# A recurrent attention with a gated feed-forward: checks of the decay weights in halves with buffers of their own, and a new table of the issue order

## The chip, the core and the metric

The kernel runs on one core of one Trainium2 chip. The core has five engines that run side by side, each through a queue of its own in order: TensorE (PE; its weight loads are listed as PEld), VectorE (DVE), ScalarE (ACT), GpSimd (POOL) and SyncE (SP), which here issues all transfers. The metric is the device time of one execution, in microseconds. Three runs of the kernel before gave 365.49 (median), 364.83 and 368.83.

## The reference

B = 4, H = 8 heads, S = 768 steps, D = 48 channels; then a feed-forward of width 1024.

```python
for t in range(S):                      # per batch and head, state is D x D
    kt, vt, rt, wt = k[:, :, t], v[:, :, t], r[:, :, t], w[:, :, t]
    cur = einsum('bhd,bhe->bhde', u * kt, vt)
    y[:, :, t] = einsum('bhd,bhde->bhe', rt, state + cur)
    state = wt[..., None] * state + einsum('bhd,bhe->bhde', kt, vt)
x = y as (B, S, H * D)
h = relu(x @ w_in); u, v = halves of h
v_n = (v - mean(v)) / sqrt(var(v) + 1e-6)
v_s = w_spatial @ v_n + b_spatial       # over the 768 steps
out = (u * v_s) @ w_out
```

## The kernel before

The 768 steps of a batch are cut into 6 chunks of 128; the 4 x 6 chunks are the slots 0 to 23. A slot turns its decays W into cumulative products with two scans on VectorE (F backwards at line 434, E forwards at line 440, which is written into a PSUM tile pa), scales k with F and r with E (lines 448 and 450), forms the 128x128 scores of all heads on TensorE (pa, line 493), copies them under a mask into As, whose diagonal holds the bonus term (line 498; the diagonal is made by line 474 on GpSimd or 479 on ScalarE), and sums its output y in PSUM (pyw, line 533): first from As and v, then from the state Sd of the slots before. The state goes on over a transposed k (pt, line 513), a product pd (line 571), two sums S0 and S1 (lines 579 and 583) and copies Sd (line 587). y is split into a high and a low part xT for the feed-forward, whose products are all made of three matmuls of such parts (`mm3`, lines 613 to 615): ph is the half v of h, pu the half u, pv the product with w_spatial, po the output. Between them lie the normalization (hv, line 680, on VectorE or ScalarE), splits into vh and vl (lines 683 and 685), and t, gh and gl (lines 719 to 724).

The weights come as raw 64-bit numbers. `split64` takes them apart: a multiplication, a shift (`low`; on VectorE line 335), a `join` (line 339) and a `sign` (line 343) on VectorE, a cast and a difference (line 351). w_spatial is split as well (lines 301 and 303).

From slot 6 on the diagonal comes from a tile N, which holds r and k of a chunk in natural order: N*N and N*u are products of lines 456 and 458, dg a sum of line 459. In slots 0 to 5 it comes from a product rk (line 414, in the same buffer N) and a small matmul pg (line 421).

The fast form is valid while no decay is over 1 and no cumulative product too small. `check_w` reads each of the 16 groups of decays once more and lets ScalarE sum what lies over 1 into a column of `over`; `range_check` at the end folds `over` and the products `prod` into one number `bad`, which decides whether a slow general form runs afterwards. With these inputs it doesn't run.

The order is no scheduler's. `Program.op` collects about 1800 operations with the engines each may run on and what it reads and writes. `plan` then takes them from a table of words PLAN: a letter for the engine (T, V, A, G, S) and the operation's number in base 36, or F and a count of filling matmuls (`warm`, line 818). The numbers beside the letters at each `op` call (0.45 for a load, say) are costs for whoever makes such a table; `plan` uses only that the letter is among them. Buffers are taken where an operation is issued; a tile whose buffer is still in use waits for its last reader. Tag N has one buffer, W, kr and v two each.

Of the kernel before, what the change touches and what calls it, by code (L numbers as in the profile page):

```python
# [19 lines left out]
G = H // 2  # L20
# [14 lines left out]
A73 S7s V6x V6y G6z G7a T7d V70 G74 S1i T3x S8u A5y T5z V7w A7e V1z A1u G28 S33 V7c T75 S7t A60 V76 V20 G1v T8b
S29 V8c A72 T61 A51 T62 V7x A52 A3y G7u V77 A7b T63 A3z G81 T7f A40 V7y A1j G82 T7g T7h A64 A65 V7z V80 V83 A7i
T7v S8v T8g V84 G8d A8e T7j V8z G86 T88 G87 A7k V1k V1l S30 S8w A8h A85 T7l Sep A53 T7m V89 A66 V1m A94 T7n A21
V90 V8a T9e G8x T8i T8j A1n A7o S3a V8f T8y V1o V97 T8k Sad G95 A7p A7q A8l V9f G9a V91 A67 A31 Seq V69 Tbd G68
V92 G6a A2a G99 V22 V93 Ses S3 A3b A35 Tal V96 G9g A9i V6b G6c Taz T8m A8n Aae G6d Tbe Vet Veu Saf Tam Tan G32
T9b S2f G6e V6f G98 Tb0 Tb1 A6g Tbr V6i Sfn Tbs V6l Aey A6j Gez V9d V9c Tbt Ab2 G6h A6m Gf4 Abu Tbf V9h G6k Aao  # L40
S3o Tfa A34 Vfb S3h T9j Aag T9k Sah T9l V36 Tg8 V37 V3c A9m V6n Vg9 A2g Sfo T8o Abg Vew T9n T8p A24 V3d G25 A9o
A38 Vev Vex T8q A8r T9p G2b S4 V3e Vfr V39 Td1 A8s T9q T9r A2m A8t S2u Vf0 G2n Aai Tcn V3j V3i A9s Tco A9t Tcp
Tdt Saj V3k Gfx S2c A9u Tf7 G9w Tdu V2h S2i V3l A3f A9v V9x A3q V3p Vfs Tdf V9y V9z Tdv Tdg A2v G3g Sgs Acq Va0
Va1 Va2 Va9 Va3 Aak G2w Ser Td2 Aaa Td3 Aa4 Tdh V3r Tb3 V3s Gab Adw Va5 Adi A2d Sgr S2x Tac Tb4 Vfu A3m V2e A3t
Ad4 Tb5 G3u Tbh Tgd V3n Tbi S2o Aa6 A2j Age Tbj Vf1 Tb6 Tbk Aa7 Tbv S2r Vf2 Vf3 Tap Taq Sfp Tbw Va8 V2k A2p Gf5
Vf8 Tbl Tar Gf6 Vft Sib A2s Vfv G2t G2q Tas Vfy A2y Sfq Gfz Gg0 Vf9 Tbx Tby Tb7 Tb8 Tbz G2z Tc0 Vb9 Tbm Vba Tat
Vc1 Tcr Vg1 Sgt Vbn Gc2 Ag3 Tau Abb Vav Tfc Vbo Abp Gfw Vgv Gga Tfd Gg4 Thc Vbq Tg5 Afe Agc Ac3 Gaw Sgu Agb Tcs
Vhd Tct Gh1 Tcu Aax Tff Vg7 Afg Vay Vbc Tcv Gc4 Tcw Tfh Gg2 Vgw Vcx Tfi Vg6 Vgx Tfj Afk Gh3 Gh4 Tch Vh5 Tci Tcj
Tck Sid Vgy Vh2 Ah7 Tgf Gh8 Vh0 Sje Tgg Tgh Sie Vcl Th9 Agz Vif Agi Vig Sic Vhe Tgj Gin Afl Afm Vhb Gio Aiq Gcy
# [137 lines left out]
def dve(n):  # L187
    return 0.157 + n / 960
# [755 lines left out]
```

## Time and profile before

| | |
|---|---|
| median of three runs | 365.49 us |
| the profiled execution | 369.64 us |
| its span, first to last instruction | 367.9 us |
| TensorE busy | 353.3 us, 3978 matmuls |
| VectorE busy | 255.7 us |
| ScalarE busy | 184.1 us |
| GpSimd busy | 165.3 us |
| DMA traffic | 47.66 MB, 130 GB/s mean |

The profile is of one execution. Matmuls are pipelined and the ends of single ones are modelled, so the distance from start to start tells more than a duration. A wait is put down to what ended last before it.

### The profile page before, as it was taken

Reading aid. Unit: us, or ns where it says so; the run is one execution under the profiler, and the core shown is the slowest. Engines: PE = TensorE matmul, PEld = TensorE weight load, DVE = VectorE, ACT = ScalarE, POOL = GpSimd, SP = SyncE. Lnnn points to the kernel's source line nnn. Section 1 sums busy time; section 2 is a strip of 40 time slices with the busy share of each in tenths; the row PEclk is TensorE's granted clock in tenths of the full one; section 3 lists DMA queues with packets and bytes.
Section 4 is the critical chain, followed back from the end, with each engine's and each line's share of the span. In section 5 each row is a group of like instructions: output and inputs, shape, how many; then the busy total and the mean of one; then the engine's idle time right before and its main releaser. Section 6 shows DMA issues by size and latency. Waiting matters only on the chain.

```text
span 367.9 us, 9774 instructions
## 1 busy us (share of the span) xinstructions
PE 353.3 (96%) x3978; PEld 324.5 (88%) x3978; DVE 255.7 (69%) x465; ACT 184.1 (50%) x482; POOL 165.3 (45%) x211
## 2 busy tenths in 40 slices
PE   7889897999999999999999999999999999999995
PEld 7766686999898988998799989999889899999994
DVE  5989998999977873788967498667696424424041
ACT  3588775874445557403465646622544564713121
POOL 5769582769557251716634164412334104114110
PEclk9999998999999999999999999999999999999998
DMA  7877767653265553352554545253404232000101
GB/s 210 249 240 201 210 203 239 205 172 116 73 201 161 154 161 131 103 151 59 142 173 122 160 142 166 69 172 87 130 2 138 66 94 79 21 23 0 62 26 70
DMA packets 30065, 47.66 MB, mean 130 GB/s; under 512 B 2896, under 2 KB 21456, under 8 KB 30016
## 3 DMA queue, kind: packets, MB, share of 16 engines
q1 hardware_dynamic: 30016, 47.00, 42.4%
q8 instruction: 32, 0.52, 0.6%
q14 instruction: 17, 0.14, 0.1%
HBM read 42.27 MB, written 4.72 MB: 128 GB/s over the span
## 4 chain that ended last, share of the span: by engine, by line
PE 75%; DVE 10%; issue 3%; DMA 1%; POOL 0%; ACT 0%; DVEq 0%; POOLq 0%; SPq 0%
PE pv L613 9%; PE pv L615 9%; PE pv L614 9%; PE pyw L533 8%; PE pa L493 5%; PE po L613 5%; PE po L615 5%; PE po L614 5%; PE pu L613 3%; PE pu L615 3%; PE pu L614 3%; PE ph L613 3%; PE ph L615 3%; PE ph L614 3%; DVE Sd L587 2%
## 5 line engine op out<-in xcount | busy, mean ns | idle before, releaser
L613 PE MATMUL pv<-ws,vh 128*128 128x384 f32 x192 | 65.0, 338 | 0.0
L615 PE MATMUL pv<-ws,vl 128*128 128x384 f32 x192 | 64.3, 335 | 0.0
L614 PE MATMUL pv<-ws,vh 128*128 128x384 f32 x192 | 64.2, 335 | 0.0
L498 DVE COPY_PREDICATED As<-mask,pa 128x512 f32<-128x512 int32 x48 | 34.6, 733 | 10.6 <-PE pa L493 8.3
L719 DVE TENSOR_TENSOR t<-pv,b_sb 128x384 f32<-128x384 f32 x32 | 17.6, 549 | 32.3 <-PE pv L615 19.9
L721 POOL TENSOR_TENSOR t<-t,us 128x384 f32<-128x384 f32 x19 | 21.1, 1113 | 37.2 <-DVE t L719 31.9
L474 POOL TENSOR_SCALAR_AFFINE_SELECT As<-dg 128x512 f32<-128x512 f32 x33 | 25.7, 785 | 26.1 <-PE pyw L533 12.7
L613 PEld LDWEIGHTS pv<-ws,vh 128*128 128x128 f32 x192 | 36.1, 188 | 0.8 <-issue 0.2
L614 PEld LDWEIGHTS pv<-ws,vh 128*128 128x128 f32 x192 | 36.1, 188 | 0.4
L615 PEld LDWEIGHTS pv<-ws,vl 128*128 128x128 f32 x192 | 36.0, 188 | 0.0
L613 PE MATMUL pu<-xT,wi 128*128 128x384 f32 x96 | 33.5, 348 | 0.0
L613 PE MATMUL po<-wo,gh 128*128 128x384 f32 x96 | 33.0, 344 | 0.0
L615 PE MATMUL pu<-xT,wi 128*128 128x384 f32 x96 | 32.4, 338 | 0.0
L615 PE MATMUL po<-wo,gl 128*128 128x384 f32 x96 | 32.3, 337 | 0.0
L614 PE MATMUL po<-wo,gh 128*128 128x384 f32 x96 | 32.3, 336 | 0.0
L614 PE MATMUL pu<-xT,wi 128*128 128x384 f32 x96 | 32.2, 336 | 0.0
L434 DVE TENSOR_TENSOR_SCAN F<-zz,W 112x512 f32<-112x512 f32 x24 | 29.1, 1215 | 3.5 <-DMA W<-in_tr_dram 1.9
L723 ACT CAST gh<-t 128x384 fp32r<-128x384 f32 x32 | 16.2, 510 | 30.1 <-POOL t L721 19.7
L440 DVE TENSOR_TENSOR_SCAN pa<-zz,W 112x512 f32<-112x512 f32 x24 | 29.4, 1223 | 0.3
L613 PE MATMUL ph<-wi,xT 128*128 128x512 f32 x72 | 29.4, 408 | 0.0
L615 PE MATMUL ph<-wi,xT 128*128 128x512 f32 x72 | 28.5, 395 | 0.7 <-DVE xT L608 0.7
L614 PE MATMUL ph<-wi,xT 128*128 128x512 f32 x72 | 28.3, 393 | 0.0
(185 smaller groups left out, 845.6 us busy)
## 6 DMA issues: line engine op xcount, KB each, us to landing
kr<-in_tr_dram SPq DMA_DIRECT2D x23, 448.0 KB, 4.3
N<-in_nat_dram SPq DMA_DIRECT2D x18, 384.0 KB, 3.3
Nw<-in_gt_dram SPq DMA_DIRECT2D x16, 384.0 KB, 3.1
W<-in_tr_dram SPq DMA_DIRECT2D x24, 224.0 KB, 3.6
v<-in_nat_dram SPq DMA_DIRECT2D x24, 192.0 KB, 3.6
out_dram<-ot SPq DMA_DIRECT2D x24, 192.0 KB, 2.0
wst<-in_w_spT_dram SPq DMA_DIRECT2D x12, 192.0 KB, 4.4
d_('wv', 0)_157<-in_w_in_dram SPq DMA_DIRECT2D x1, 512.0 KB, 7.2
```

The lines of the kernel that those rows point to most:

```text
L434: op({"V": 1.24}, lambda: nc.vector.tensor_tensor_scan(flat(F()[:R])[:, ::-1], flat(zz[:R])[:, ::-1], flat(W())[:, ::-1], 0.0, ALU.max, AL ...
L440: op({"V": 1.24}, lambda: nc.vector.tensor_tensor_scan(flat(E()[:R]), flat(zz[:R]), flat(W()), 0.0, ALU.max, ALU.mult), r=[(W, 0), ("zz", ...
L474: e.affine_select(out=As(), in_=dg()[:, j::2].unsqueeze(2).broadcast_to([P, G, C]), pattern=[[0, G], [1, C]], compare_op=ALU.is_equal, fil ...
L493: nc.tensor.matmul(pa[j]()[:, g, :], kk()[rs, g, :], rr()[rs, g, :], start=True, stop=True)
L498: op({"V": 0.725}, lambda j=j, As=As: nc.vector.copy_predicated(As(), mask.unsqueeze(1).broadcast_to([P, G, C]), pa[j]()), r=[(pa[j], 0)], ...
L533: nc.tensor.matmul(py()[Q * n:Q * (n + 1), k_, :], a, b, start=n not in started, stop=not left[0], skip_group_check=True)
L613: nc.tensor.matmul(ps, ah, bh, start=first, stop=False)
L614: nc.tensor.matmul(ps, ah, bl, start=False, stop=False)
L615: nc.tensor.matmul(ps, al, bh, start=False, stop=last)
L719: op({"V": dve(HT)}, lambda: nc.vector.tensor_tensor(t1(), pv()[:, :HT], b_sb[:, tsl], ALU.add), r=[(pv, 0), ("b", 0)], w=[(t1, 0)])
L721: op({"V": dve(HT), "G": pool(HT)}, lambda e: e.tensor_tensor(t1(), t1(), us(), ALU.mult), r=[(us, 0)], w=[(t1, 0)], port=True)
L723: op({"A": act(HT)}, lambda: nc.scalar.copy(gh(), t1()), r=[(t1, 0)], w=[(gh, 0)])
```

## The change

Three things. First, `check_w` loads each group as two halves of 128 x 384 in place of one of 128 x 768, into a tag of its own, Nw, with two buffers in another pool, and checks each half by itself; `over` has 32 columns for it. In the program's list a group's check now follows one of the slots 7 to 22, one group to a slot, and no longer comes in fours behind the last slot of a batch; the table places the halves where it likes. Second, some costs beside operations have other values. Third, the table is new from its first word to its last, with other engines for some operations.

```diff
-    over = cp.tile([P, B * G], F32, name="over")
+    over = cp.tile([P, 2 * B * G], F32, name="over")
...
     def check_w(n):
-        w = buf(p2, [P, 2, DM], "N", f"Nw{n}", 1)
-        def flat():
-            return w().rearrange("p a d -> p (a d)")
-        load(w, [0], lambda: nc.sync.dma_start(flat(), gt[n, :, 0, :]), P * S * 4)
-        op({"A": 1.03}, lambda: nc.scalar.activation(flat(), flat(), AF.Relu, bias=neg, accum_out=over[:, n:n + 1]),
-           r=[(w, 0)], w=[(w, 0), ("over", n)])
+        for h in range(2):
+            w, m = buf(pm, [P, HT], "Nw", f"Nw{n}_{h}", 2), 2 * n + h
+            load(w, [0], lambda w=w, h=h: nc.sync.dma_start(w(), gt[n, :, 0, h * HT:(h + 1) * HT]), P * HT * 4)
+            op({"A": 0.7}, lambda w=w, m=m: nc.scalar.activation(
+                w(), w(), AF.Relu, bias=neg, accum_out=over[:, m:m + 1]), r=[(w, 0)], w=[(w, 0), ("over", m)])
...
-        op({"T": 0.89}, mm, r=[(kr, 0), (kr, 1)], w=[(pa[0], 0), (pa[1], 0)], mode="rows")
+        op({"T": 0.98}, mm, r=[(kr, 0), (kr, 1)], w=[(pa[0], 0), (pa[1], 0)], mode="rows")
...
+        if 0 < i - B_PE <= B * G:
+            check_w(i - B_PE - 1)
         if c == NC_ - 1:
-            for g in range(G):
-                check_w(b * G + g)
...
-T0 Sq Vw Vx Vy A11 Sr Ss S2 St S1 S41 S42 S5 A15 Gu S43 G12 Fd Tv A14 S54 Vz V13 F3 T18 A10 V46 A16 G17 V19 T1b
+Sq Sr Ss S1 T0 Vw Gu A11 S2 S41 Vx Vy G12 Fb Tv St S5 Vz S42 S43 A14 S54 V13 G16 G17 A10 G15 V46 F3 T18 V19 T1b
```

Three places of the order. In the names the first number of As, kr, pa, F, W and dg is the slot; hv and vl carry batch and chunk. In the changed file, lines behind `check_w` have numbers smaller by 3, lines between the table and `check_w` larger by 1.

VectorE, from the E scan of slot 5 to the masked copies of slot 5, before:

```order
L440 SCALAR_TENSOR_TENSOR pa5_0_885<-zz_80,W5_612 112x512
...
L450 TENSOR_TENSOR kr5_744<-kr5_744,pa5_0_885 112x4x127
L667 TENSOR_TENSOR st0_0_667<-st0_0_667 128x3
L434 SCALAR_TENSOR_TENSOR F6_934<-zz_80,W6_786 112x512
L438 RECIPROCAL zz_80<-F6_934 112x4
L680 TENSOR_SCALAR hv0_0_674<-hv0_0_674,st0_0_667 128x512
L680 TENSOR_SCALAR hv0_1_666<-hv0_1_666,st0_0_667 128x512
L680 TENSOR_SCALAR hv0_2_719<-hv0_2_719,st0_0_667 128x512
L498 COPY_PREDICATED As5_1_883<-mask_103,pa5_1_947 128x512
L498 COPY_PREDICATED As5_0_901<-mask_103,pa5_0_885 128x512
L587 COPY Sd_113<-S1_112 48x4x48
```

and now:

```order
L437 SCALAR_TENSOR_TENSOR pa5_0_945<-zz_80,W5_644 112x512
L677 TENSOR_SCALAR hv0_0_590<-hv0_0_590,st0_0_591 128x512
L447 TENSOR_TENSOR kr5_701<-kr5_701,pa5_0_945 112x4x127
L677 TENSOR_SCALAR hv0_1_606<-hv0_1_606,st0_0_591 128x512
L584 COPY Sd_113<-S1_112 48x4x48
L453 TENSOR_TENSOR N6_885<-N6_885 128x384
L495 COPY_PREDICATED As5_0_950<-mask_103,pa5_0_945 128x512
L336 TENSOR_SCALAR d_('wo', 1)_834<-d_('wo', 1)_834 128x384
L495 COPY_PREDICATED As5_1_926<-mask_103,pa5_1_965 128x512
L336 TENSOR_SCALAR d_('wo', 2)_904<-d_('wo', 2)_904 128x384
L456 TENSOR_REDUCE dg6_1019<-N6_885 128x8
L431 SCALAR_TENSOR_TENSOR F6_1023<-zz_80,W6_775 112x512
```

The F scan of slot 6 has moved behind the copies of slot 5; two hv stand apart in place of three together; Sd, N*N of slot 6 and a shift have come in front of the last copy.

GpSimd at the same place, before:

```order
L303 TENSOR_TENSOR ws1_122<-wst5_1_775,ws0_121 128x384
L670 TENSOR_TENSOR st0_0_667<-st0_0_667 128x3
L466 COPY vp1_116<-v5_777 128x4x2x16
L448 TENSOR_TENSOR kr6_889<-kr6_889,F6_934 112x4x127
L685 TENSOR_TENSOR vl0_0_990<-hv0_0_674,vh0_0_966 128x512
L466 COPY vp0_115<-v6_905 128x4x2x16
L685 TENSOR_TENSOR vl0_1_1000<-hv0_1_666,vh0_1_981 128x512
```

and now:

```order
L667 TENSOR_TENSOR st0_0_591<-st0_0_591 128x3
L471 AFFINE_SELECT As5_0_950<-dg5_868 128x512
L304 TENSOR_TENSOR ws1_122<-wst2_1_758,ws0_121 128x384
L682 TENSOR_TENSOR vl0_0_977<-hv0_0_590,vh0_0_952 128x512
L455 TENSOR_TENSOR N6_885<-N6_885,u_sb_107 128x384
L682 TENSOR_TENSOR vl0_1_1008<-hv0_1_606,vh0_1_974 128x512
L471 AFFINE_SELECT As6_1_1041<-dg6_1019 128x512
L445 TENSOR_TENSOR kr6_937<-kr6_937,F6_1023 112x4x127
```

The product on kr6 has moved from the front of both vl to behind them, and N6 comes between the vl.

SyncE's queue, where the first checks are loaded, before:

```order
L375 DMA W6_786<-in_tr_dram 112x4x128
L310 DMA d_('wo', 1)_841<-in_w_out_dram 128x768
L392 DMA Nw0_876<-in_gt_dram 128x768
L378 DMA kr6_889<-in_tr_dram 112x1024
L383 DMA v6_905<-in_nat_dram 128x384
L846 DMA u_sb_107<-in_u_rep_dram 128x384
L392 DMA Nw1_937<-in_gt_dram 128x768
```

and now:

```order
L376 DMA W5_644<-in_tr_dram 112x4x128
L389 DMA Nw6_0_648<-in_gt_dram 128x384
L384 DMA v4_657<-in_nat_dram 128x384
L379 DMA kr5_701<-in_tr_dram 112x1024
L843 DMA u_sb_107<-in_u_rep_dram 128x384
L384 DMA v5_753<-in_nat_dram 128x384
...
L376 DMA W6_775<-in_tr_dram 112x4x128
...
L383 DMA N6_885<-in_nat_dram 128x768
```

A half of group 6 is loaded first, a slot earlier than a check was before, and N6 is loaded before any other check stands in the queue.

## Rows read from the trace of the kernel before

**Rows 1.** Busy time by windows: window, then PE, PEld, DVE, ACT, POOL, clock, DMA

```profile
30.00:40.00 10.00, 8.12 (x131) 5.91 (x127) 9.94 (x13) 6.76 (x21) 7.86 (x9) 1.00 0.70 205
100.00:150.00 50.00, 50.00 (x592) 45.36 (x589) 34.55 (x69) 28.98 (x78) 22.84 (x34) 1.00 0.53 157
```

**Rows 2.** TensorE's waits: engine, line, releaser; total us, times, longest

```profile
PE pyw L533 <- DVE As L498: 4.6, 3, 2.7
...
PE pyw L818 <- ACT xT L606: 0.6, 1, 0.6
```

**Rows 3.** Timeline, VectorE, then TensorE: start, us, engine, line, operation [idle before]

```profile
51.99 5.33 DVE L680 TENSOR_SCALAR hv<-hv,st 128x512 f32<-128x512 f32 x3
57.25 1.32 DVE L498 COPY_PREDICATED As<-mask,pa 128x512 f32<-128x512 int32 x2
...
58.62 0.66 PE L533 MATMUL pyw<-As,v 128*32 128x128 f32 x8 [2.69 <-DVE As L498]
```

**Rows 4.** Timeline of GpSimd meanwhile, first and last of the four

```profile
53.08 1.27 POOL L448 TENSOR_TENSOR kr<-kr,F 112x508 f32<-112x508 f32 x1
...
55.78 1.26 POOL L685 TENSOR_TENSOR vl<-hv,vh 128x512 fp32r<-128x512 f32 x1
```

**Rows 5.** Granted clock in tenths, forty slices; two pieces of the chain (start, us)

```profile
PEclk9999998999999999999999999999999999999998
...
58.62 3.21 PE pyw L533 x56
...
97.73 1.67 PE pyw L533 x56
```

**Rows 6.** Timeline of TensorE around a change of matmul form; a transposition in the chain

```profile
50.60 0.33 PE L614 MATMUL pu<-xT,wi 128*128 128x384 f32 x1
50.78 0.34 PE L615 MATMUL pu<-xT,wi 128*128 128x384 f32 x1
51.05 1.16 PE L493 MATMUL pa<-kr 48*128 48x128 f32 x16
...
76.77 0.39 PE pt L513 x4
```

**Rows 7.** VectorE by groups (count, busy us, mean ns, idle before); two rows of its timeline

```profile
L434 DVE TENSOR_TENSOR_SCAN F<-zz,W 112x512 f32<-112x512 f32 x24 | 29.1, 1215 | 3.5 <-DMA W<-in_tr_dram 1.9 <-POOL kr L448 0.7 <-issue 0.6
L587 DVE COPY Sd<-S 48x192 f32<-48x192 f32 x18 | 12.4, 691 | 0.8 <-POOL S L583 0.5
L680 DVE TENSOR_SCALAR hv<-hv,st 128x512 f32<-128x512 f32 x13 | 11.7, 922 | 0.0
L438 DVE RECIPROCAL zz<-F 112x4 f32<-112x4 f32 x24 | 4.3, 178 | 0.2
L456 DVE TENSOR_TENSOR N<-N 128x384 f32<-128x384 f32 x6 | 3.9, 651 | 3.2 <-DMA N<-in_nat_dram 3.2
L583 DVE TENSOR_TENSOR S<-S,prod 112x192 f32<-112x192 f32 x6 | 2.6, 438 | 0.0
...
42.08 0.40 DVE L335 TENSOR_SCALAR d_('wu', 0)_607<-d_('wu', 0)_607 128x512 int32<-128x512 int32 x1
59.23 0.56 DVE L339 SCALAR_TENSOR_TENSOR e_('wo', 0)_910<-e_('wo', 0)_910,d_('wo', 0)_623 128x384 int32<-128x384 int32 x1
```

**Rows 8.** The check on ScalarE (ns least, median, most); SyncE's waits for its buffer

```profile
L393 ACT ACTIVATE Nw<-Nw,neg x16: 923/936/944, 52.0 to 333.2; 128x768 f32<-128x768 f32 x16
L393 ACT ACTIVATION_READ_ACCUMULATOR Nw<-Nw,neg x16: 182/186/209, 52.9 to 334.0; 128x1 f32 x16
...
SPq L392 <- ACT Nw L393: 28.8, 10, 3.9
```

**Rows 9.** Timeline of VectorE: first, longest and last of ten lengthened instructions

```profile
13.91 0.97 DVE L339 SCALAR_TENSOR_TENSOR e_('wv', 0)_267<-e_('wv', 0)_267,d_('wv', 0)_157 128x512 int32<-128x512 int32 x1
...
32.88 2.28 DVE L339 SCALAR_TENSOR_TENSOR e_('wu', 2)_537<-e_('wu', 2)_537,d_('wu', 2)_445 128x512 int32<-128x512 int32 x1
...
46.27 1.57 DVE L351 TENSOR_TENSOR wi<-e_('wu', 0)_696,wi 128x512 fp32r<-128x512 f32 x1
```

More of the change, by code (lines that the diff above doesn't have):

```diff
@@ L35 @@
[L35 to L49, printed above, removed]
@@ new lines @@
+Sy7 Vl9 Tnh Vqj Tja Gqv Al4 Tni Tmb Tmc Ajb Ale Vke Tnj Vqk Tmd Ank Vl8 Gqp Vql Tkf Ay8 Ame Vqm Vqo Vqq Tkg Tkh
+Vrs Vld Gdy Vqn Vrt Vru Tlf Gqu Vrk Gqw Tlg Srj Aki Grv Vrl Ssn Tlh Ali Akj Grw Tqx Tr0 Vr1 Vlj Vqz Srh Tdz Te0
+Ssp Te1 Grq Grp Vqy Vrm Avh Ajc Te2 Tlk Ajd Tll Tlm Sub Su7 Tr2 Aln Vrn Vrr Grx Tr3 Ts1 Vs2 Try Alo Gs3 Vs0 Ar4
+Akk Tor Tos Vr5 Gsz Vrz Alp Alq Vlr Gt0 Tot Tr6 Vls Aou As5 Glt Teb Sso Vlu Tr7 Glv Glw Vlx Vt1 Tec Aly Vm4 Ted
+Gt3 Am5 Te5 Sud Am1 Ve3 Te6 Se4 Te7 Tr8 Am2 Vm3 Alz Vm6 Gm0 Gun Tee Swn Te8 Aef Ar9 Vs4 Tmf Ara Au8 Tmg Tmh Tmi
@@ new lines @@
+T197 T10a T101 V10b A18d Ssl V19b V18e T17a A194 A195 T102 T103 T104 T11n T11o T11p T11q T11r T11s T119 V105
+G19c T11a V198 S106 A19e A19d G15u G15v T10v Asm V11t V15w V15x V15y A164 T10w T10x T10y G196 V199 Sm7 A161 A162
+A17b A17c A17d T10z T110 V163 A15z G160 T11b T11c T11d T11e V111 T19f T19g T19h G11u A19i T10r V10q V19j T10s
+T10t A11v A10u V11f T1al T19k G11w A165 T19l T19m T18f T18g A19n G11g T18h T129 A11h V11i A19o A19p G112 T1am
+T1a7 A113 A18i T1an V114 T12a A18j A18k S10c T1a8 T1a9 A1aa T11x T12b A19q T1d1 A1ao T1d2 T1d3 A1d4 V19s G19t
@@ new lines @@
+G19r G19u V19v T123 G19w V19x A1a1 A1a4 A1a5 V166 G1a6 A19y T11y T11z T120 T124 A1a2 A121 T125 V1a3 T12c A19z
+G1a0 A17h S14j T126 V127 T1ab T1b3 A12d T1b4 T1b5 S122 S128 A14k S12e T1bh Sm9 T1az T1ac T1ad T1ae T1af T1b0
+T1b1 T1b6 T1ag A1b2 T1ap T1aq T1ar T1bi T1bj T1bk V1ah T1bl T1b7 T1bm T1b8 T1cn T1as T1co G1ai V1b9 V1bn T1at
+V1bo A1bp V1bq A1aj T1cp T1df G1ak T1au V1av A1cq T1c9 Ama T1ca V1aw A1ax V1ay T1c3 T1cd T1ce T1dg V1ba A1bb
+T1cf T1cg V1bc T1dh A1di T1c4 T1cb T1br T1c5 A1cc T1c6 T1bs T1bx T1bt T1bu Am8 V1ec A1c7 T1by S1c8 T1ch T1ci
@@ L99 @@
+V1cj T1bz T1c0 T1dj T1dk V1ck T1dl A1cl T1dm T1cr G1cm T1cs A1bv S1bw T1dn T1do V1dp T1d5 G1dq T1ct T1cu T1cv
+A1dr T1cw V1cx V1cy V1ds T1d6 A1cz V1d0 T1d7 T1d8 T1d9 A1c1 S1c2 T1da T1e5 T1e6 T1dz T1e0 V1db V1dc A1dd V1de
+T1dt T1du T1dv T1dw T1e1 V1dx T1e2 S1dy T1e7 T1e8 A1e3 S1e4 V1e9 A1ea T1ed S1eb V1ee
 """
@@ L343, in sign @@
             V.scalar_tensor_tensor(m, dh, -2**31, m, ALU.bitwise_and, ALU.bitwise_or)
-        op({"A": act(n), "V": one}, rebias, r=[(d, 0)], w=[(em, 0)], port=True)
-        op({"A": act(n), "V": one}, low, w=[(d, 1)], port=True)
+        op({"A": act(n) + 0.06, "V": one}, rebias, r=[(d, 0)], w=[(em, 0)], port=True)
+        op({"A": 0.2 + n * 0.00114, "V": one}, low, w=[(d, 1)], port=True)
         op({"V": two}, join, r=[(d, 1)], w=[(em, 0)], port=True)
@@ L465, in slot_prep @@
         vp = q["vp"] = vps[i % 2]
-        op({"A": 0.3, "G": 0.68}, lambda e: (e.copy if e is nc.scalar else e.tensor_copy)(
+        op({"A": 0.3, "G": 0.3}, lambda e: (e.copy if e is nc.scalar else e.tensor_copy)(
             vp.rearrange("p g (a b) -> p g a b", b=T)[:, :, 0::3],
@@ L831, in low @@
             nc.vector.tensor_tensor(okr[:, 0:1], okr[:, 0:1], okr[:, 1:2], ALU.min)
-        op({"V": 0.9}, low, r=[("over", i) for i in range(B * G)] + [("Wc", i) for i in range(NS)] + [("S1",)],
+        op({"V": 0.9}, low, r=[("over", i) for i in range(2 * B * G)] + [("Wc", i) for i in range(NS)] + [("S1",)],
            w=[("okr",)] + [("Wc", i) for i in range(NS)])
```

122 lines of the change are left out of this document (60 added, 62 removed).

## The prediction

> **What bounds the kernel now.** I read the table by windows first. From 100 to 150 us TensorE is busy for 50.00 of 50 us while VectorE has 34.55; from 30 to 40 us it is VectorE that is full, 9.94 of 10 [rows 1]. So the kernel has two parts. In the first sixty microseconds the weights are still being split, and the decay scans, the masked copies and the splitting share VectorE; TensorE gets its inputs as fast as VectorE makes them. After that TensorE runs without pause to the end, so whatever the first part loses is lost for good, and whatever it gains is kept.
>
> Then the waits of TensorE, and the largest says it directly: 4.6 us in 3 waits for the masked copies As of line 498, the longest 2.7 [rows 2]. The timeline shows that one: TensorE stands still for 2.69 us and begins again at 58.62, when the two copies As of slot 5 are done. VectorE is not idle meanwhile. Its three normalizations hv of line 680 take 5.33 us together, and As follows only at 57.25 [rows 3]. An undisturbed one is far shorter: the group has 13 with 11.7 us busy [rows 7], and the ten others make (11.7 - 5.33)/10 = 0.64 us. What holds them is beside it on GpSimd: from 53.08 to 57.04 it goes through four operations without a pause, from 1.27 us on kr to a vl of 1.26 us, and VectorE gets on only behind the last [rows 4]. I call this a hold: a VectorE instruction whose operands are ready stands while GpSimd works.
>
> The stall costs twice. The page's row of granted clock, forty slices of 9.2 us, has an 8 in the seventh, which holds the stretch behind the stall, and again at the very end; all others are nines [rows 5]. In the chain the 56 small matmuls behind the stall take 3.21 us, and the same 56 take 1.67 us at 97.73 [rows 5]: TensorE worked at 1.2 GHz there and not at 2.4. The two other waits for As, 1.9 us together, did not do that. So this episode cost 2.69 + (3.21 - 1.67) = 4.2 us.
>
> The profiled execution took 369.64 us, 367.9 in its span and 1.74 around it; the median of the three runs is 365.49. Without the episode the profiled one would be at 365.4. I take it that the median runs lack it, or have it small, and that one of the three (368.83) had one.
>
> **The change part by part.** *The check loads.* Sixteen checks of 768 columns become thirty-two of 384. One now takes 0.94 us on ScalarE and 0.19 us for reading its accumulator [rows 8], 18 us in all. A half has at least half the first and the whole second, 0.66, and at most what it has now; 32 of them are 21 to 36 us. ScalarE is busy for half the span, and TensorE's longest wait for it is 0.6 us [rows 2], so I count nothing; without that cover it would be 3 us at the lower end. The buffers: SyncE waited 28.8 us in 10 waits until a check had freed the common N buffer [rows 8], and the loads of W, kr and v stood behind it in the one queue. The halves wait for each other only. A gain needs TensorE to wait for such a load, and its waits show none, so nothing again. Sixteen more issues fall to SyncE, which computes nothing.
>
> *The costs written beside the operations* are read by no one when the order comes from the table: nothing.
>
> *The table, VectorE up to the As copies of slot 5.* This is where TensorE's longest stall ended, so I count what VectorE has to do until then in either order. New in front of them: three shifts of line 335, one join and one sign of the 384-wide weights, one product N*N, one state product S. Gone: the scan F of slot 6, one copy Sd, one of the three hv and three short ones. By rows [rows 7]: 3 x 0.40 + 2 x 0.56 + 0.65 + 0.44 = 3.4 us come, and 1.21 + 0.69 + 0.64 + three of at most 0.18 = 3.0 go. These means hold average holds already. VectorE has +0.4 us more.
>
> *The table, TensorE up to the same place.* In front of As5 it has done one transposition and one third of a projection (three matmuls) less. The transposition is 0.39 us; matmuls start 0.17 us apart, so the third is 0.52 [rows 6]. These 0.9 us are still to do when it is let go: +0.9.
>
> *Changes between full matmuls and the small tiled ones.* The last full matmul before the small ones at 51.05 takes 0.27 us from start to start, others 0.17 [rows 6]: 0.1 us per change. The orders have 91 and 88 changes: -0.3.
>
> *Filling matmuls.* 31 in place of 28, all in the first 25 us, where TensorE is ahead of VectorE. I count nothing; with no cover, three of two passes of a tenth of a microsecond would be 0.6.
>
> *The long hold.* Before, three hv stand together, and behind them on GpSimd the product on kr6, a vl, a copy and the other vl are all ready. Now two hv remain there, with the product on kr5 between them; the kr6 product has moved behind As5, and GpSimd has one mask diagonal, one difference ws and one vl, after which its next product needs N6 from VectorE. So it must pause. The price lies between 0 (as long a hold) and -4.2 (gone). I take it as gone: the queue that filled those four microseconds isn't there any more.
>
> *Other holds.* From 13.9 to 46.3 us ten instructions of VectorE that read and write SBUF are longer than the shortest of their kind, from the join of 0.97 at 13.91 over one of 2.28 at 32.88 to a difference of 1.57 at 46.27, by 6.3 us in all [rows 9]. Which operation meets which is decided by tenths of a microsecond, and the new order deals all of them anew. I take the same sum; between none (-6.3) and double (+6.3) nothing is excluded.
>
> *The end.* Both orders close with the same steps: last output group, two half copies, store, check matmul. Nothing.
>
> Sum: 369.64 - 4.2 + 0.4 + 0.9 - 0.3 = 366.4 us, 0.3% over the median shown.
>
> **Rivals.** *The long hold comes back (slower).* Behind hv, Sd and N*N in the new order GpSimd can have a diagonal, ws and vl ready in a row, about 0.6 + 1.0 + 1.3 = 2.9 us, and the As copies of slot 5 stand behind all of them. For it: four instructions that can be held stand there in front of As5, where there were three. Against it: vl needs hv and a ScalarE cast first. It decides once TensorE stands as long as it did before 58.62, near 2.7 us; then the clock falls as well and the whole episode is back: 366.4 + 4.2 = 370.6 us. Slower also if the scan of slot 6, now behind As5, comes late: I count 6.0 us of VectorE work up to the next score matmul against 6.6 of TensorE work, so only 0.6 us of cover.
>
> *More instructions, more holds (slower).* The new order has five more long VectorE instructions with SBUF on both sides in front of As5 (three shifts, join, sign, N*N and S come, one Sd and one hv go). If each finds GpSimd in the middle of an operation like the 1.26 us vl [rows 4], with its busy share of 0.79 [rows 1], it loses 0.63 x 0.79 = 0.5 us, together 2.5: 368.9 us. For it: the ten holds are of that size. Against it: the shift at 42.08 took 0.40 us and the join at 59.23 0.56, no more than other undisturbed ones [rows 7]. The Trainium skill, SBUF — State Buffer, section "SBUF: two separate sides", states the rule behind this rival: VectorE and GpSimd take one pair of ports in turn as an exclusive lock, whoever starts first for its whole instruction, and the other one blocks. The trace agrees that VectorE stands while GpSimd works, and differs in the length: the long hold lasted over four instructions of GpSimd, not over one.
>
> *The holds shrink (faster).* If the new interleaving halves the 6.3 us, TensorE is let go 3.1 us earlier: 363.3. For it: more operations on ScalarE (copies Sd, the first check) keep out of the quarrel. Against it: GpSimd's work in front of As5 is the same within half a microsecond. To be faster by 1% three quarters of the holds have to go.
>
> *The check's buffers do what they are for.* If the loads behind SyncE's waits were what VectorE's waits for N and kr hang on, these vanish: 3.2 us for N in six products [rows 7]. TensorE waited for none of it, so at most the last microsecond could be won: 365.4.
>
> **How the numbers follow.** Forecast 366.4 with a chance of 0.44; the long hold returns 0.18 (370.6); more holds 0.13 (368.9); the holds shrink 0.2 (363.3); the check's buffers pay 0.05 (365.4). One per cent, about what a measurement of this kernel can tell from no change, is 361.8 to 369.1. Slower by more: the first rival and a good third of the second, 0.23. Faster by more: somewhat over half of the shrinking holds, 0.12. Between: 0.65. The range goes from 362.3, where two thirds of the holds are gone, to 370.8, the returned episode; some 0.1 are left out on each side. The likeliest case's own range is 364.5 to 368.5.
>
> **What would show it.** Right: As5 done on VectorE between 54 and 57 us; TensorE's waits for As in the first sixty microseconds under 3 us in total; granted clock at full level from the first ten microseconds to the end; behind that TensorE without pauses as before; no ScalarE or SyncE wait of TensorE through a check. The step on hv is wrong if any hv or Sd takes over 2 us before As5; the step on work is wrong if TensorE waits for the scores of slot 6 or 7; the step on the checks is wrong if TensorE waits for a load. The prediction falls if the stretch behind 60 us, and not the one before it, differs by more than 1 us between the two kernels.

## The result

The changed kernel takes 371.3 us in the median of 20 runs (370.07 to 373.95), the kernel before 368.06 in the median of its 20 runs (364.56 to 370.61): a ratio of 1.0121 with a 95% interval of 1.0096 to 1.0146, slower by 1.2% (by the two medians alone 0.9%). I had said 366.4, with a range up to 370.8 and 0.23 for slower by more than 1%. The runs of before lie six microseconds apart, some near 365 and most between 367 and 370; those of the changed kernel lie closer together.

### The profile page after: what moved, and what is told of

It reads as the page before. It is cut to its first block, busy times and chain, and to the rows that moved or that the text cites. A ratio compares the mean times of both kernels' runs of the same rounds, so it can differ in the third digit from the quotient of the medians.

```text
span 371.8 us, 9821 instructions
## 1 busy us (share of the span) xinstructions
PE 355.9 (96%) x3984; PEld 327.8 (88%) x3984; DVE 251.2 (68%) x461; ACT 186.9 (50%) x504; POOL 165.7 (45%) x216
## 4 chain that ended last, share of the span: by engine, by line
PE 72%; DVE 7%; POOL 3%; issue 2%; ACT 1%; POOLq 0%; DVEq 0%
PE pv L610 9%; PE pv L611 9%; PE pv L612 9%; PE pyw L530 7%; PE pa L490 5%; PE po L610 5%; PE po L612 4%; PE po L611 4%; PE ph L610 3%; PE pu L610 3%; PE ph L611 3%; PE ph L612 3%; PE pu L612 3%; PE pu L611 3%; PE pt L510 1%
## 5 line engine op out<-in xcount | busy, mean ns | idle before, releaser
L720 ACT CAST gh<-t 128x384 fp32r<-128x384 f32 x32 | 16.2, 510 | 47.4 <-DVE t L718 34.7
L471 POOL TENSOR_SCALAR_AFFINE_SELECT As<-dg 128x512 f32<-128x512 f32 x36 | 27.0, 756 | 22.7 <-PE pyw L530 12.1
L445 POOL TENSOR_TENSOR kr<-kr,F 112x508 f32<-112x508 f32 x22 | 26.3, 1196 | 23.9 <-PE ph L612 8.3
L490 PE MATMUL pa<-kr 48*128 48x128 f32 x384 | 28.8, 291 | 3.2 <-DVE dg L459 1.7
L490 PEld LDWEIGHTS pa<-kr 48*128 48x128 f32 x384 | 24.2, 193 | 7.6 <-issue 4.5
L610 PE MATMUL ph<-wi,xT 128*128 128x512 f32 x72 | 30.0, 417 | 0.0
L437 DVE TENSOR_TENSOR_SCAN pa<-zz,W 112x512 f32<-112x512 f32 x24 | 29.4, 1226 | 0.4
```

Source lines behind the costliest of these rows:

```text
L437: op({"V": 1.24}, lambda: nc.vector.tensor_tensor_scan(flat(E()[:R]), flat(zz[:R]), flat(W()), 0.0, ALU.max, ALU.mult), r=[(W, 0), ("zz", ...
L445: op({"V": dve(508), "G": 1.1}, lambda e: e.tensor_tensor(kk()[:, :, :C - 1], kk()[:, :, :C - 1], F()[:R, :, 1:], ALU.mult), r=[(F, 0)], w ...
L471: e.affine_select(out=As(), in_=dg()[:, j::2].unsqueeze(2).broadcast_to([P, G, C]), pattern=[[0, G], [1, C]], compare_op=ALU.is_equal, fil ...
L490: nc.tensor.matmul(pa[j]()[:, g, :], kk()[rs, g, :], rr()[rs, g, :], start=True, stop=True)
L610: nc.tensor.matmul(ps, ah, bh, start=first, stop=False)
L720: op({"A": act(HT)}, lambda: nc.scalar.copy(gh(), t1()), r=[(t1, 0)], w=[(gh, 0)])
```

## The profile after

The profiled execution took 373.48 us, its span is 371.8. It is not a typical one: it lies 2.2 us over the median, and only two others of the twenty (371.94 and 373.95 us) were granted as little of TensorE's clock, 0.991 of it or less over the span. Three had all of it and still took 370.07 to 371.24 us, so the low clock shown here is not what makes the median slow. The page's row of the granted clock, as in [rows 5]:

```profile
PEclk9978999999999999999999999999999999999999
```

The dip behind the long hold, in the seventh slice of before, is gone. A new and longer one is in the third and fourth, from 18 to 37 us. TensorE's waits, as in [rows 2] (engine, line, releaser; total us, times, longest):

```profile
PE pyw L530 <- issue: 1.8, 1, 1.8
PE pa L490 <- DVE dg L459: 1.7, 1, 1.7
PE pa L490 <- DVE kr L447: 1.2, 2, 0.7
PE pv L611 <- POOL ws L304: 0.7, 1, 0.7
PE pyw L530 <- DVE As L495: 0.7, 1, 0.7
```

The wait for As has fallen from 4.6 us to 0.7. In its place stand waits for scores (pa; dg stands in VectorE's queue behind the product kr, which is what the scores read), for a low part ws, and one of 1.8 us that waits for nothing the profile shows. Busy time by windows of the changed kernel, as in [rows 1]:

```profile
15.00:30.00 15.00, 13.20 (x235) 10.91 (x225) 13.86 (x22) 10.31 (x26) 9.80 (x12) 0.80 0.73 228
30.00:45.00 15.00, 13.21 (x259) 10.18 (x260) 11.97 (x21) 10.21 (x28) 9.04 (x11) 0.97 0.64 185
45.00:60.00 15.00, 13.76 (x211) 11.71 (x211) 14.68 (x24) 12.58 (x33) 13.79 (x19) 1.00 0.77 214
60.00:75.00 15.00, 14.09 (x118) 12.64 (x119) 13.88 (x22) 10.07 (x28) 13.15 (x15) 1.00 0.69 206
75.00:90.00 15.00, 13.60 (x145) 12.74 (x145) 13.92 (x25) 11.50 (x33) 12.58 (x12) 1.00 0.61 178
```

and the same windows of the kernel before:

```profile
15.00:30.00 15.00, 12.87 (x287) 9.57 (x287) 13.75 (x23) 11.54 (x26) 11.57 (x12) 1.00 0.83 253
30.00:45.00 15.00, 13.12 (x221) 9.89 (x217) 14.79 (x24) 10.85 (x33) 10.95 (x12) 1.00 0.70 204
45.00:60.00 15.00, 12.28 (x205) 10.74 (x197) 14.87 (x23) 10.49 (x26) 10.54 (x16) 0.95 0.72 225
60.00:75.00 15.00, 15.00 (x145) 13.65 (x137) 13.53 (x29) 11.14 (x31) 8.01 (x8) 0.93 0.66 202
75.00:90.00 15.00, 15.00 (x152) 14.65 (x152) 14.66 (x23) 8.01 (x20) 12.59 (x13) 1.00 0.48 140
```

Two things are to be seen. From 30 to 45 us VectorE, which sets the pace there, works 11.97 us where it worked 14.79: it waits. From 15 to 60 us it is idle for 4.49 us in all, before for 1.59. From 60 to 90 us TensorE is idle for 0.91 + 1.40 = 2.31 us, where before it was not idle at all.

To compare kernels whose orders differ I add up TensorE's work in the order in which it starts, each kind at its steady distance from start to start (0.174 us for a matmul of pu, pv or po, 0.231 for ph, 1.09 for a slot's scores, 0.39 for its transpositions, 0.030 for each small one of y, 0.01 for each of pd and pg; fills count nothing; 330.1 us in all). The table says how late TensorE is, start time less work, when so much work is done. Each column is one profiled execution.

| work done, us | before | changed | old_As5_first | old38_new | old104_new | new36_old | new_kr1_first |
|---|---|---|---|---|---|---|---|
| 10 | 15.6 | 19.6 | 13.8 | 13.9 | 14.4 | 17.1 | 14.8 |
| 25 | 19.9 | 23.4 | 18.9 | 19.0 | 19.6 | 22.4 | 21.3 |
| 40 | 25.5 | 26.2 | 20.8 | 22.2 | 21.3 | 23.9 | 23.4 |
| 60 | 26.0 | 29.4 | 22.0 | 27.7 | 22.6 | 25.2 | 26.5 |
| 80 | 26.8 | 29.8 | 22.9 | 28.1 | 24.2 | 26.0 | 27.1 |
| 330 | 33.1 | 36.9 | 29.1 | 35.2 | 33.1 | 33.1 | 34.1 |

Ten units are done at 26 to 30 us, sixty at 86 to 89 in the first two. The changed kernel loses 4.0 us to before in its first ten units. Before loses 5.6 us between 25 and 40 units, where its long hold lies and the changed kernel loses 2.8, and so they are nearly level at 40. From 40 to 60 the changed kernel loses 3.2 us, before 0.5. Of the 3.8 us between the two at the end, 0.7 are there at 40 units and 3.1 come behind.

## The experiments

The kernels before that ran on the same chips had medians from 367.0 to 368.5 us; so a difference between kernels that ran on different chips is not known to better than about 1 us. "Old" and "new" are the tables of before and of the change; lines are those of the changed file. The edits are shortened, those of the tables told in words.

### The checks

checks_alone, the old table with the half checks, and nochk_new, the new table without checks:

```diff
-S Nw0            A Nw0
+S Nw0_0 S Nw0_1  A Nw0_0 A Nw0_1
...
-            check_w(i - B_PE - 1)
+            pass
```

> The order of the kernel before, with the half checks in buffers of their own: each load of a group is replaced by its two half loads at the same place, each check by its two half checks. Theory A, the order alone makes the change slower: TensorE waits for no check, so this stays within 0.7 us of the kernel before (368.1 in the median of its 20 runs). Theory B, the sixteen additional checks and loads cost what was lost: 371.3 us, as the changed kernel.

> The changed kernel with its table, but without the checks of the decay weights (neither their loads nor their sums; the columns they would fill are set to zero). Theory A, the order alone: within 0.7 us of the changed kernel's 371.3. Theory B, the checks cost it, through ScalarE or through the loads in SyncE's queue: 368.1, the time of the kernel before.

Measured: 368.61 (365.1 to 370.14; ratio to before 1.0025, 0.9986 to 1.0063) and 371.66. The checks are not it. Later, with the long hold out of the way:

> The kernel before with its full-size checks in the common buffer, and the one move of the copies of slot 5. It differs from the kernel with 365.8 us in the checks alone, without the long hold that spreads the runs of before. If halves and buffers of their own cost or bring nothing: 365.8 within 0.5. If the halves cost ScalarE's 3 us or more somewhere on the path: 363 to 364.5. If the separate buffers pay: 367 or more.

365.02 (ratio to before 0.9944, 0.9909 to 0.9979), against 365.77 with halves: if anything the halves cost 0.7 us, less than the runs of either spread.

### The long hold of the old order

```diff
+V As5_1
+V As5_0
 V hv0_0
 V hv0_1
 V hv0_2
-V As5_1
-V As5_0
```

> The order of the kernel before with the half checks (its time was that of before, 368.6 in the median, from 365.1 to 370.1), and one move: VectorE makes the two masked copies of slot 5 in front of the three normalizations hv and no longer behind them, as their operands are ready at 52.2 us. Theory H (my prediction's: TensorE's stall in front of 58.6 us is the price of VectorE being held, and it is in most runs of before): the stall of 2.7 us and the lower clock behind it vanish, 368.6 - 3 to 4 = 364.6 to 365.6, and the runs lie close together. Rival: what holds hv then holds the copies or what follows, and TensorE waits a little later instead: 367.5 to 369.

Measured: 365.77, from 364.75 to 367.65 (before on the same chip 367.89). Timeline of VectorE, then of TensorE, of this kernel, as in [rows 3]:

```profile
51.22 1.38 DVE L495 COPY_PREDICATED As<-mask,pa 128x512 f32<-128x512 int32 x2 [0.16 <-PE pa L490]
52.48 1.69 DVE L677 TENSOR_SCALAR hv<-hv,st 128x512 f32<-128x512 f32 x3
...
55.52 0.43 PE L530 MATMUL pyw<-As,v 128*32 128x128 f32 x8
```

The copies are done at 52.6 us, six microseconds earlier, TensorE does not wait for them, and the three hv now take 1.69 us, not 5.33. The hold was real, and its price in the median is 2 to 3 us: 2.1 beside before on the same chip, 2.8 beside checks_alone on another, 3.0 with full checks (365.02 beside 367.98). That it is also what spreads the runs of before is likely and not shown: with full checks and the move they still go from 363.85 to 368.87. The kernel with full checks and this one move (365.02) beats both kernels of this case.

The same rule at slot 3 (As3 in front of Sd and a sign):

> The old order with the copies As of slot 5 in front of hv (365.8 us), and the same move for slot 3: its two copies come directly behind the join of the fifth block of w_in, which is held for 2.30 us, and in front of the copy Sd (1.24), the sign (0.99) and two short ones. In the trace TensorE waits 0.66 and 1.23 us for these copies. If what stands in front of a copy is what TensorE pays for, most of the 1.9 us goes and is kept to the end: 364.0, within 0.7. Rival, Sd and the weights that come later make TensorE wait as long: 365.8.

Measured: 366.51. Nothing was won, where 1.1 to 2.5 us had been expected. The two waits for As3 are gone, and in their place stands this one of TensorE:

```profile
39.83 1.46 PE L490 MATMUL pa<-kr 48*128 48x128 f32 x16 [1.25 <-DVE kr L447]
```

Behind it TensorE is at 1.2 GHz for 3.4 us. What was put off came in front of the next scores. There VectorE has no slack (14.76 of 15 us busy from 30 to 45 us in old_As5_first), and an order can only choose what is late.

### Where along the table

```diff
-PLAN = the new table
+PLAN = the old table's first 201 (513, 601) words, then what is left in the new order
...
+PLAN = the new table's first 179 words, then what is left in the old order
```

> The changed kernel with the issue order of the kernel before for the first 201 words (up to the y of slot 3, some 38 us), and behind them the new order of what is left. Theory A1, the loss lies in the start: the same TensorE work is done 3.0 us later by 25 us and 4.2 us later by 50 us in the changed kernel's trace than in that of before, so this gives 371.3 - 3 to 4 = 367 to 368.3. Theory A2, it lies behind the start, in the scores of slots 6 to 8 and later: 371 to 372.

> The same with the order of the kernel before for its first 513 words (up to the state product of slot 7, some 88 us), then the new order. Theory A1 and A2 both: the loss is in front of that place, and what the new order loses behind it is under 1 us by the two traces, so 368.1 to 369. If the loss lies behind 88 us (theory A3): 371.3.

> The old order with the masked copies of slot 5 in front of hv (365.8 us) for its first 601 words, up to some 100 us, then the new order; the half checks stand where the old order has its checks. Theory L, the new order loses its time in front of that place, and behind it as little as the traces say (7.5 us against 7.1 from the sixtieth microsecond of TensorE work to the end): 366.2, within 0.8. Rival, it is lost over the whole length, by more changes of form, holds or loads: 369 or more.

> The reverse: the new order for its first 179 words, up to some 36 us, then that same old order. At that place the new order has done its TensorE work 3 to 5 us later than the old one. Theory P, a late start is passed on to the end, as TensorE hardly waits in the old order behind 58 us: 365.8 + 3 to 5 = 369 to 371. Theory S, VectorE's queue up to 58 us sets the pace and swallows a late start: 366 to 367.5; then the loss of the new order lies between 36 and 100 us.

Measured: old38_new 372.46, old88_new 373.55, old104_new 368.68, new36_old 371.34. The first two missed, and old104_new missed its 366.2 by 2.5 us and comes near its rival; new36_old is at the late end of theory P. The first two have a stall of their own. In old88_new TensorE waits for 1.9 us at 94 us, at the seam, and the old hold is in it as well. In old38_new the sign of a block of w_out is held; VectorE, then GpSimd meanwhile:

```profile
61.13 4.07 DVE L344 SCALAR_TENSOR_TENSOR e_('wo', 1)_943<-d_('wo', 1)_835,e_('wo', 1)_943 128x384 int32<-128x384 int32 x1
...
60.64 0.95 POOL L471 TENSOR_SCALAR_AFFINE_SELECT As<-dg 128x512 f32<-128x512 f32 x1
61.57 2.00 POOL L304 TENSOR_TENSOR ws<-wst,ws 128x384 fp32r<-128x384 f32 x2
63.53 1.25 POOL L682 TENSOR_TENSOR vl<-hv,vh 128x512 fp32r<-128x512 f32 x1
```

It stands from 61.13 to 65.20 us while GpSimd goes through a diagonal, two differences and a vl, and the scores of slot 6 stand behind it. (The profile puts TensorE's 2.69 us there down to a check's load, but with the product kr6 in front of the sign, in old38_kr_first below, the wait is gone.) So the new order has a long hold too, and whether it strikes depends on what GpSimd is doing just then.

new36_old holds 1.8 us that no other kernel has, behind TensorE's last instruction (SyncE pauses there between its last two drains; for what, the profile doesn't show), and a wait of 2.76 us at its seam. If each of its runs has that pause (one was traced), it would be 369.5 without it. old104_new says that behind 100 us the new order costs 2.9 us more than the old one if it gets there early: TensorE stands five times for 0.8 to 1.0 us from start to start, for xT, Sd, ph, xT and ot. The changed kernel, which gets there late, has two of these (Sd, ot). So the losses do not add up: the new start with its seam costs 3.7 us over 365.8 (without the pause at the end), middle and end 6.7 (with the hold of 4.07), the end alone 2.9, and all together 5.5. That TensorE's lateness from one place covers the waits of the next would explain it; beyond these waits it is not shown.

### The start

Chain of the changed kernel at 21 to 32 us: timelines of TensorE, ScalarE, GpSimd and VectorE:

```profile
20.98 0.85 PE L530 MATMUL pyw<-kr,Sd 112*32 112x128 f32 x20
23.61 0.41 PE L530 MATMUL pyw<-kr,Sd 112*32 112x128 f32 x4 [1.78 <-issue]
23.95 2.08 PE L490 MATMUL pa<-kr 48*128 48x128 f32 x16
...
27.96 0.48 ACT L603 CAST xT<-pyw 128x384 fp32r<-128x384 f32 x1 [2.90 <-PE pyw L600]
28.54 0.62 ACT L350 CAST wi<-e_('wv', 2)_454 128x512 fp32r<-128x512 f32 x1
...
29.24 1.31 POOL L352 TENSOR_TENSOR wi<-e_('wv', 2)_454,wi 128x512 fp32r<-128x512 f32 x1 [2.73 <-ACT wi L350]
30.49 1.30 POOL L411 TENSOR_TENSOR rk<-kr 112x512 f32<-112x512 f32 x1
...
31.82 0.16 DVE L439 TENSOR_TENSOR kr<-kr,zz 112x4 f32<-112x4 f32 x1 [1.88 <-POOL rk L411]
```

TensorE stops in the middle of 24 small matmuls, goes on at 1.2 GHz (the scores take 2.08 us, not 1.16), ScalarE waits 2.90 us for it, GpSimd 2.73 us for ScalarE, VectorE 1.88 us for GpSimd. From this come 1.8 of VectorE's 3.03 us of idle time between 30 and 45 us; another 1.1 are a wait for the scores of slot 3. How long this ring waits differs from run to run: in the four other traces with the same start (nochk_new, new_kr_first, new_noV, new_noG) VectorE is idle for 0.1 to 1.9 us from 30 to 45 us, and for 2.3 to 3.9 from 15 to 60.

Where a kernel has this stop, it is at the same count of TensorE's instructions (matmuls, weight loads and the few of its sequencer), behind the 705th that the trace lists. Times of five kernels, from their traces:

| kernel | 449th starts | last start ahead of it | second packet starts | goes on |
|---|---|---|---|---|
| before | 15.38 | 21.62 | 20.06 | 22.57 |
| changed | 17.84 | 21.56 | 21.06 | 23.61 |
| nochk_new | 18.52 | 22.32 | 22.13 | 24.56 |
| new_kr_first | 18.30 | 22.02 | 21.94 | 24.28 |
| old_As5_first | 15.03 | 20.69 | 18.12 | no stop |

The packets are those of the instruction queue, 32 of 16 KB in the page (0.52 MB) for TensorE's 7968 matmuls and loads. TensorE goes on 2.3 to 2.6 us after the second one starts. In the new start it runs through the 256 instructions from the 449th in 3.7 us, in the old one in 5.6 to 6.2. Whether it stops hangs on when that packet starts: 3.2 to 4.7 us after the 449th instruction in the four that stop, 3.1 in old_As5_first, which runs through more slowly. The Trainium skill, Runtime: NRT & Kernel Launch, section "Instruction fetch mechanics", says that such blocks of 256 are fetched while the one before is executed and that the cost of a crossing is mostly hidden; here it is 1.78 us in the open. Two kernels move the boundary, by tiny fills that cost instructions and little time (72 passes in 2.4 and 1.1 us):

```diff
-F 11
+F 8, then 36 of 32 x 2
...
-F 11
+F 9, then 36 of 32 x 2 in the four quarters in turn
```

> The changed kernel with another first group of filling matmuls: 8 in place of 11, and behind them 36 tiny ones (32 x 2 elements), before TensorE's first real work at 7.3 us. Each fill is four instructions of TensorE (two passes, each with a load of weights), so all that follows stands 132 instructions further on in its stream. In the traces TensorE stops for 0.7 to 2.0 us at one and the same count of its instructions, behind the 705th, and goes on 2.4 to 2.6 us after the second of the 16 KB packets of the instruction queue has started. Theory F, it waits for its own instructions, since it goes through a block of 256 faster than the next is brought: the boundary now falls behind what was the 573rd, where TensorE is slower, and the stop of 1.8 us and the low clock behind it (24.0 to 30.8 us) vanish: 371.3 - 2 to -3 = 368.3 to 369.3. Rival, it stands at that place of the program for another reason: the stop stays with the same matmul at 22 us, and the time is 371.3.

> The changed kernel with 9 fills in its first group in place of 11, and 36 tiny ones behind them that go to the four quarters of the array in turn (the small products of this kernel run four times as fast in that form). All that follows stands 136 instructions further on. In the first such try the stop at 22 us was gone, but the tiny fills took 2.4 us and TensorE was at the low clock from 9.3 to 16.2 us, so the time told nothing. Theory F: no stop at 22 us, full clock from 24 to 31 us, and of the 1.8 + 3.4 us at least 1 stays to the end: 369 to 370.3. Theory W, the start's loss is swallowed by the waits for VectorE and GpSimd behind it: 371.3 within 0.5, and TensorE's waits from 55 to 90 us grow by what was won.

Measured: 373.53 and 373.46. In both the stop is gone from its place. Timeline of TensorE of new_fetch2, its first scores and the 24 small matmuls that were cut in two:

```profile
9.60 2.08 PE L490 MATMUL pa<-kr 48*128 48x128 f32 x16
...
24.13 0.86 PE L530 MATMUL pyw<-kr,Sd 112*32 112x128 f32 x24
```

The first row is why the time tells nothing: TensorE is at 1.2 GHz for these scores, which take 2.08 us where at the full clock they take 1.16. In new_fetch2 the full clock is granted from 15.0 us on, in the changed kernel from 6.9; in new_early_fetch it is granted at 5.9, falls at 9.3 behind the tiny fills and is back at 16.2. So in new_fetch2 the scores of slot 1 start 3.2 us later than in the changed kernel and those of slot 2 still 1.0 later. The cause of the stop is shown, its price is not.

A move on VectorE for slot 1:

```diff
+V kr1 (product with E)
 V sign of the first block
-V kr1 (product with E)
```

> The changed kernel with one move: VectorE's product of r and E of slot 1 stands in front of the sign of the first block of w_in, which was held for 1.47 us. The scores of slot 1 can start some 1.3 us earlier (16.4 us in the trace). Theory F, a start won is kept: 371.3 - 0.7 to -1.3 = 370.3. Theory W, it is swallowed (here by TensorE reaching the stop at its 705th instruction earlier, whose next block comes no earlier, or by the waits behind): 371.3 within 0.5.

Measured: 370.55 (ratio to before 1.0093, 1.0059 to 1.0127), and the second packet came at 18.7 us, in time, without a stop, though TensorE runs through the 256 instructions as fast (3.6 us). The move itself did little, as the scores of slot 1 start at 16.22 us and not at 16.42; that the packet started 1.0 us behind the 449th instruction and not 3.2 is what helped, and no run shows why it did. TensorE is 4.8 us less late at 10 units, and less than the kernel before; it is 2.8 less late at 40, and still 2.8 at the end. In the medians 0.75 us is left: the changed kernel's traced run is itself 2.2 us over its median. So 2 us of the start are swallowed by 40 units, and 0.75 to 3 reach the end.

One wait no run here moved. It is the 1.7 us for dg in the list above, in front of the scores of slot 4. Timeline of VectorE, then TensorE, of the changed kernel:

```profile
42.47 1.66 DVE L344 SCALAR_TENSOR_TENSOR e_('wu', 2)_641<-d_('wu', 2)_515,e_('wu', 2)_641 128x512 int32<-128x512 int32 x1
44.05 0.67 DVE L447 TENSOR_TENSOR kr<-kr,pa 112x508 f32<-112x508 f32 x1
...
44.87 1.16 PE L490 MATMUL pa<-kr 48*128 48x128 f32 x16 [1.70 <-DVE dg L459]
```

The product kr stands behind a sign that takes 1.66 us here. TensorE waits 1.7 us at this place in seven traces of the new order and 2.3 in new_fetch2, where the sign takes 0.68; before has no such wait. What it costs at the end is open.

### The middle

```diff
+V kr6 (product with E)
 V join, V sign of wo1
-V kr6 (product with E)
...
+V kr7 (product with E)
 V ws, V hv, V hv
-V kr7 (product with E)
```

> The changed kernel with two moves on VectorE: the product of r and E of slot 6 stands in front of the join and the sign of the third set of weights (both were lengthened, 1.24 and 1.27 us), that of slot 7 in front of a difference and two hv (2.8 us). Theory A, VectorE's order in this stretch costs TensorE its waits for the scores of slots 6 and 7 (0.8 and 1.1 us from start to start in place of 0.3): both go, 371.3 - 1.2 = 370.1, within 0.5. Rival: what was put off (the weights, hv) makes TensorE wait as long a little later: 371.3 or more.

> The kernel with the old order up to 38 us and the new one behind it (372.5), with the same two moves. In its trace the sign of the weights was held for 4.07 us beside three differences ws on GpSimd, and TensorE stood 3.03 us in front of the scores of slot 6, with the lower clock behind. Theory A: a TensorE input behind an instruction that can be held is what costs; with the product in front of it the whole episode goes, 372.5 - 4.5 - 0.5 = 367.5, within 0.8. Rival: the hold falls on another instruction that TensorE waits for: 370 or more.

Measured: 371.08 and 371.71. The waits for the scores of slots 6 and 7 are gone from the first but for 0.3 us and the 4.07 us hold from the second, and neither gains more than 0.8: in the first the wait at ws stays (1.10 us from start to start), in the second TensorE stands at the scores of slot 7 and at ws (1.19 and 1.52). So I took work away.

```diff
+LEAVE: V join and V sign of wo1, wo2, wo3
...
+G memset in place of the difference: six ws, three wo
```

> The changed kernel without the joins and signs of three of the four blocks of w_out (their weights have wrong low bits and signs then): six instructions of VectorE that take 7.2 us in all from 64 to 81 us of its trace. Theory V, VectorE's backlog between 58 and 88 us is what TensorE waits for there (it loses 3.6 us against its work between 52 and 89 us): 371.3 - 2 to -3 = 368.3 to 369.3. Rival G, GpSimd's queue is (it is busy for 25.7 of the 30 us from 60 to 90): 370.7 or more.

> The changed kernel with nine differences on GpSimd replaced by fillings with zeros (the low parts of six blocks of w_spatial and of three of w_out are zero then): 1.0 to 1.4 us each become some 0.3. Theory G, GpSimd's queue between 58 and 88 us is what TensorE waits for, by itself or by holding VectorE: 371.3 - 2 to -3 = 368.3 to 369.3. Rival V, VectorE's own work is: 370.7 or more.

Measured: 369.39 and 369.72. Windows, new_noV, then new_noG:

```profile
60.00:75.00 15.00, 15.00 (x108) 13.59 (x98) 11.46 (x22) 11.68 (x33) 14.23 (x16) 1.00 0.76 232
75.00:90.00 15.00, 15.00 (x155) 14.53 (x154) 13.55 (x22) 9.62 (x28) 11.26 (x11) 1.00 0.61 168
```

```profile
60.00:75.00 15.00, 14.48 (x94) 13.11 (x87) 13.47 (x23) 11.54 (x31) 11.81 (x17) 1.00 0.75 224
75.00:90.00 15.00, 15.00 (x155) 14.53 (x154) 13.65 (x27) 10.00 (x29) 8.66 (x10) 1.00 0.63 178
```

With less on either engine TensorE's 2.31 us of idle time go to 0 and 0.52, and the kernel is 1.9 and 1.6 us faster by the medians; by the ratios to before on their own chip (1.0064, 1.0035 to 1.0092, and 1.0090, 1.0055 to 1.0124) 2.1 and 1.1, and the second interval overlaps that of the changed kernel. The traces bear it out: nochk_new, within 0.5 us of both at 40 units of work, is 2.4 and 2.1 us later than they at the end. Neither rival wins: the two engines wait for each other. In the changed kernel's timeline GpSimd, in front of the ws that TensorE waits for, stands 2.34 us for a sum dg of VectorE:

```profile
81.69 2.09 POOL L471 TENSOR_SCALAR_AFFINE_SELECT As<-dg 128x512 f32<-128x512 f32 x1 [2.34 <-DVE dg L456]
83.75 1.01 POOL L304 TENSOR_TENSOR ws<-wst,ws 128x384 fp32r<-128x384 f32 x1
...
84.81 0.44 PE L611 MATMUL pv<-ws,vh 128*128 128x384 f32 x1 [0.67 <-POOL ws L304]
```

## Why the prediction was wrong

**The long hold.** Right in its mechanism: no hv takes over 2 us in front of As5, and moving the copies in the old order removes stall and low clock. Timeline of VectorE of the changed kernel, as in [rows 3]:

```profile
55.26 0.54 DVE L677 TENSOR_SCALAR hv<-hv,st 128x512 f32<-128x512 f32 x1
55.83 0.95 DVE L584 COPY Sd<-S 48x192 f32<-48x192 f32 x1
56.82 1.55 DVE L453 TENSOR_TENSOR N<-N 128x384 f32<-128x384 f32 x1
...
59.64 0.72 DVE L495 COPY_PREDICATED As<-mask,pa 128x512 f32<-128x512 int32 x1
```

But As5 is done at 60.4 us and not between 54 and 57. The hold's size was read off one held run, 4.2 us; in medians the move of As5 is worth 2.1 to 3.0. Also wrong was the reading of the three runs: the median of before over twenty is 368, not 365.5, and both traces of that order (before and checks_alone) have the hold.

**VectorE up to As5, +0.4 us.** This is the first step that failed. I counted what VectorE has to do and took it that it never waits in this part. By the sum As5 would have been done at 58.57 - 3.4 (the hold, 5.33 - 3 x 0.64) + 0.4 = 55.6 us; it is done 4.8 us later. In the old order VectorE hardly waits (0.2 us idle of 15 from 30 to 45 us). In the new one it is idle for 3.03 of these 15, most of it at the end of a ring through TensorE, ScalarE and GpSimd, and from 15 to 60 us for 2.9 us more than before, in the four other traces for 0.7 to 2.3 more. The count of instructions was right and told nothing of this.

**Fills and the first 25 us, 0.** I put the start at nothing, as TensorE is ahead of VectorE there. It loses 4 us by 10 units of work, through the stop for instructions and 6.8 us at the low clock (24.0 to 30.8 us): new_kr1_first, without either, is ahead of before there. My sign that the clock would be full from 10 us on failed here. That 0.75 to 3 us of it reach the end is all that the runs say.

**Behind As5, nothing.** This is the second step that failed. I saw that the cover in front of slot 6's scores is 0.6 us and gave it no price. TensorE waits 0.49 and 0.73 us for the scores of slots 6 and 7 and 0.67 for ws, which by my own sign makes the step on work wrong; the idle 2.31 us are worth about 2 (new_noV, 1.9 to 2.4). My rule that the prediction falls if the stretch behind 60 us differs by over 1 us applies: from 40 units to the end the table's traces give 7.6 us for before and 10.7 for the change.

**TensorE's work, forms, checks, end.** TensorE's +0.9 and the forms' -0.3 are too small to be seen. The checks at nothing hold within 0.7, though the halves take 25.6 us of ScalarE where the whole ones took 18.0. No wait of TensorE is for a load.

**More holds, halved holds.** Neither rival was it. Counting what instructions take over the shortest of their form, where that is over 0.1 us, VectorE's work is lengthened by 25 us in the changed trace and by 28 in that of before: the new order has less holding and is slower. The Trainium skill's rule, SBUF — State Buffer, section "SBUF: two separate sides", that VectorE and GpSimd lock a common pair of ports for a whole instruction, agrees in kind with the hold in old38_new (4.07 us beside four GpSimd instructions); as before the length is that of several instructions, not of one.

In sum: 366.4 + 1.9 for the middle and 0.75 to 3 for the start makes 369 to 371.3, a sum made up afterwards. What is open is the share of the instruction stop, of the wait for the scores of slot 4, and why the new order behind 100 us has three more waits when it gets there early.

## What to carry to other kernels

Count idle time of the engine that sets the pace, not only its work: a new order of the same work can make it wait in a ring of engines that no single wait shows. Put what TensorE waits for in front of instructions that a neighbour can hold, but only where the engine has slack behind; otherwise the wait moves to the next slot. A part of a table that is good by itself is not good behind another start: try halves of two orders together before a loss is put down to one place.

## What the runs showed of the hardware

TensorE can wait for its own instructions: after 256 of them, gone through in 3.7 to 6.2 us, it comes to a boundary that is served 2.2 to 2.7 us after its packet starts, and stands there for 0.4 to 2.0 us; eight kernels show it at one count, it leaves the place when the count is moved, and it is not there when the packet starts early (new_kr1_first, 1.0 us). A stop of 1.8 us can bring TensorE to 1.2 GHz for 6.8 us (changed kernel) or not at once (nochk_new, 2.0 us, clock full there). One instruction of VectorE was held for 4.07 us over four of GpSimd. And with two or three full fills fewer at the start and 36 tiny ones behind them the first scores took 2.08 us and not 1.16.
